# Fewer, wider small operations in a decode kernel with attention and MLP: remainder products, masks, bias row and quadrant copies

## The chip, the cores and the metric

The kernel runs on one core of a Trainium2 chip. The metric is the device time of one execution in microseconds (us), the median of several runs. Five engines work side by side, each through a fixed list of instructions: TensorE (PE, with weight loads as PEld), VectorE (DVE), ScalarE (ACT), GpSimd (POOL) and SyncE (SP), which here only issues transfers. They wait for each other through semaphores. Transfers from memory (HBM) to the on-chip buffer are issued on queues and moved by 16 DMA engines.

## What is computed

A decode step for 8 sequences: attention over the last 2048 positions of a cache of keys and values (32 query heads, 16 key/value heads of 128), an MLP with a hidden width of 4608, and a gate that mixes the two. From the reference, cut to what matters:

```python
def _A_ref(x, k_cache, v_cache, wq, wo):          # x: 8 x 1 x 576
    W = min(4096, max(256, Sk // 4))              # Sk = 8192, W = 2048
    q = (x @ wq).reshape(B, Sq, Hq, Dh)...        # wq: 576 x 4096
    k = jnp.repeat(k_cache[:, :, Sk - W:, :], rep, axis=1)
    v = jnp.repeat(v_cache[:, :, Sk - W:, :], rep, axis=1)
    scores = jnp.einsum("bhqd,bhkd->bhqk", q, k) * (Dh ** -0.5)
    p = _softmax(scores, axis=-1)
    o = jnp.einsum("bhqk,bhkd->bhqd", p, v)
    return ... @ wo                               # wo: 4096 x 576

def _B_ref(x, w1, b1, w2, b2):
    y = _layernorm(x, axis=-1)
    h = _gelu(jnp.einsum("bsd,df->bsf", y, w1) + b1)   # w1: 576 x 4608
    return jnp.einsum("bsf,fd->bsd", h, w2) + b2       # w2: 4608 x 576

x = A_x
g = _sigmoid((x * gate_w).sum(-1, keepdims=True))
return g * a + (1 - g) * b
```

The parts of the cache that are read are 8 x 16 x 2048 x 128 values of two bytes, 67.1 MB of keys and as much of values. The four weights are 20.1 MB together.

## The kernel before

The program is written as a plan: each operation is added with its engine, what it depends on, and an estimated cost. A small list scheduler inside the program uses the estimates to fix the order of each engine's list. Semaphore waits are then made from the dependencies.

```python
def add(self, eng, fn, deps=(), name=None, cost=0.1, after=(), prio=0): ...
def dma(self, eng, fn, semkey, nbytes, deps=(), name=None, after=(), prio=0): ...
# schedule(): of the ready operations, take the least (earliest start - 0.2 * prio, -prio, index)
    if op.is_dma:
        eng_free[op.eng] = est + op.cost                    # DMA_ISSUE = 0.35
        if op.nbytes < 65536:
            op.t1 = est + 0.4 + self.DMA_LAT                # DMA_LAT = 1.8: thought to be done at t1
        else:
            start = max(est + 0.4, dma_free)
            dma_free = start + op.nbytes / self.DMA_BW      # DMA_BW = 428e3 bytes per us
            op.t1 = dma_free + self.DMA_LAT
    else:
        op.t1 = est + op.cost                               # an operation may start 0.08 after what it needs
```

The inner dimension 576 is 4 x 128 + 64. The 64 rows that remain of wq and w1 are loaded two to a row pair, so that the two halves of the output columns lie on even and odd partitions; the input's remainder columns are spread with zeros to match (`xT[:, 4]` serves the first half of the heads, `xT[:, 5]` the second). Each block of 128 outputs takes five products:

```python
def q_fn(e):
    for hq in range(Hq):                                   # 32 heads
        out_ = ps[:, BK_Q, hq * 8: hq * 8 + 8]
        for t in range(4):
            ins = e.matmul(out_, wq_m[:, t, hq * 128:(hq + 1) * 128], xT[:, t, :], start=(t == 0), stop=False)
        c = hq % 16
        ins = e.matmul(out_, wq_r[:, c * 128:(c + 1) * 128], xT[:, 4 + hq // 16, :], start=False, stop=True)
# w1: the same, 36 blocks, weights read with a stride of 9, in lists of 6 blocks
o_hch.append(add("pe", fn, deps=dw1 + [o_yT], name="h_pe%d" % len(o_hch), cost=0.06 * 5 * len(fts), after=o_hch[-1:]))
```

Masks are made on VectorE before the inputs land: `own` by five memsets, `i2` by a memset and four copies, `i32` by four copies from an identity matrix.

The softmax of a group finds the maximum of 128 partitions x 512 scores (L597), brings the maxima of the four partition quadrants together (L600), and takes their maximum in three operations (L601 to L603):

```python
m01 = add("dve", ... max(k(MX), k(GA)) ...)
m23 = add("dve", ... max(k(GB_), k(GC_)) ...)
tt  = add("dve", ... max(k(M01), k(M23)) ...)
```

Keys come in 16 loads of 4.19 MB (`k_unit`), alternating between two buffers. A buffer is free when the two transposes of its content (L666) are done. Values come in 32 loads of 2.10 MB (`v_unit`) through five buffers, each free when its products (L711) are done. All these loads go out from SyncE in one fixed order:

```python
order = ("0 1 v 2 v 3 v 4 v v 5 v v 6 v v 7 v v 8 v v 9 v v 10 v v 11 v v 12 v v 13 v v 14 v 15 "
         "w w v v w w v v v v v v b m m m m")     # numbers: K; v: V; w: wo; b: output bias; m: w2
```

The products of a V load have the name `pv0` to `pv31`; item n holds `pv` 2n and 2n + 1. After each pair of V loads an item of attention output is evicted by ScalarE (L722), summed (L728), evicted again (L738) into one of two small buffers, scaled by GpSimd (L749), and at the end brought into place for the products with wo, by copies between partition quadrants (L761). The last four items have a burst of 16 copies each:

```python
ev = add("act", ... activation(out=o32[:, item % 2, :], in_=osrc, func=ACTF.Copy),
         deps=[prev] + ([oT_done[2 * item - 4], oT_done[2 * item - 3]] if item >= 2 else []), ...)
if i == NUQ - 9:
    place(slice(0, 8), slice(0, 6), list(oT_done.values()))
elif i >= NUQ - 8:
    c = (i % 8) // 2
    place_done[c] = place(slice(c, 8, 4), slice(6, 8), [oT_done[i - 1], oT_done[i]])

def place(ch, bs, deps):
    return [add("dve", ... tensor_copy(oT[32 * q:32 * q + 32, ch, j, bs], oN[32 * j:32 * j + 32, q, ch, bs]) ...)
            for j in range(4) for q in range(4)]
...
AccGroup("proj%d" % c, mms, place_done[c] + ds, cost=1.1)          # four groups, c = 0..3, 16 products each
```

The output bias b2 is loaded to 8 partitions and multiplied by a diagonal 8 x 8 matrix of 1 - g, split in a high and a low part (`ob`):

```python
o_obh = add("dve", lambda e: e.tensor_copy(ob[:, 0:8], dg[:, 8:16]), deps=[o_dgb], ...)
d = dma("sp", lambda e: e.dma_start(b2_sb, B_b2.partition_broadcast(8)), "b2", 65536, name="d_b2", after=last_dma[-1:])   # 65536: nbytes
o_m2.append(AccGroup("m2_b", [(ob[:, 0:8], b2_sb), (ob[:, 8:16], b2_sb)], [d, o_obl, o_obh], cost=0.6).op)
```

A w2 load needs a buffer that V products have freed: the four of them come after `pv27`, `pv28`, `pv29` and `pv30`. The group of wo products (`proj`) and those of w2 and b2 add up in one bank of PSUM; ScalarE evicts the half that wo and b2 have used when all of these groups are done (L807).

The last load of w2 comes in four pieces; their products (L555), one addition (L826) and the store of the output (L827) end the kernel.

Of the kernel before, what the change touches and what calls it, by code (L numbers as in the profile page):

```python
# [173 lines left out]
def held_matmul(nc, e, out, lhsT, rhs, start=False, stop=True, skip=False, tile_size=(128, 128), tile_position=(0, 0)):  # L174
    return e.add_instruction(mybir.InstMatmult(
        name=nc.get_next_instruction_name(), engine=mybir.EngineType.PE,
        ins=[e.lower_ap(rhs), e.lower_ap(lhsT)], outs=[e.lower_ap(out)],
        start_tensor_calc=start, stop_tensor_calc=stop, is_transpose=False, bass_skip_group_check=skip,
        tile_size=tile_size, tile_position=tile_position, ldweights=False))


def build_kernel(nc, A_x, A_k_cache, A_v_cache, A_wq, A_wo, B_x, B_w1, B_b1, B_w2, B_b2, gate_w, out):
# [24 lines left out]
    with ExitStack() as es:  # L207
# [39 lines left out]
        req("o32", 2 * 16, F32)  # L247
# [57 lines left out]
        b2_sb = view("b2", 8)  # L305
        u_sb, uh_sb, v1_sb, v2_sb = view("u"), view("uh"), view("v1"), view("v2")
        hT = view("hT").rearrange("p (t b) -> p t b", b=8)
        ob = view("ob", 8)
        ot32 = view("ot32", 8)
# [5 lines left out]
        o32 = view("o32").rearrange("p (u m) -> p u m", u=2)  # L315
# [60 lines left out]
        o_own0 = add("dve", lambda e: e.memset(view("own"), 0.0), name="own0", cost=0.1)  # L376
        o_own = [add("dve", (lambda a=a: lambda e: e.memset(view("own")[32 * a:32 * a + 32, a:a + 1], 1.0))(), deps=[o_own0], name="own%d" % a, cost=0.1) for a in range(4)]
# [67 lines left out]
        def b1ev_fn(e):  # L445
# [8 lines left out]
        o_obh = add("dve", lambda e: e.tensor_copy(ob[:, 0:8], dg[:, 8:16]), deps=[o_dgb], name="ob_hi", cost=0.12)  # L454
        o_ob32 = add("dve", lambda e: e.tensor_copy(ot32, ob[:, 0:8]), deps=[o_obh], name="ob_32", cost=0.12)
        o_obl = add("dve", lambda e: e.tensor_tensor(out=ob[:, 8:16], in0=dg[:, 8:16], in1=ot32, op=ALU.subtract), deps=[o_ob32], name="ob_lo", cost=0.12)

        o_i32 = []
        o_i20 = add("dve", lambda e: e.memset(view("i2"), 0.0), name="i2z", cost=0.1, prio=-1)
        o_i2 = [add("dve", (lambda q=q: lambda e: e.tensor_copy(i2[32 * q:32 * q + 32, :, q // 2, :], ident[32 * q:32 * q + 32, 32 * q:32 * q + 32].rearrange("p (r m) -> p r m", r=4)))(),  # L460
                    deps=[o_i20, o_ident], name="i2_%d" % q, cost=0.15, prio=-1) for q in range(4)]
        for q in range(4):
            o_i32.append(add("dve", (lambda q=q: lambda e: e.tensor_copy(i32[32 * q:32 * q + 32, :], ident[32 * q:32 * q + 32, 32 * q:32 * q + 32]))(),
                             deps=[o_ident, o_obl], name="i32_%d" % q, cost=0.15, prio=-1))


        def q_fn(e):
            ins = None
            for hq in range(Hq):
                out_ = ps[:, BK_Q, hq * 8: hq * 8 + 8]  # L470
                for t in range(4):
                    ins = e.matmul(out_, wq_m[:, t, hq * 128:(hq + 1) * 128], xT[:, t, :], start=(t == 0), stop=False)
                c = hq % 16
                ins = e.matmul(out_, wq_r[:, c * 128:(c + 1) * 128], xT[:, 4 + hq // 16, :], start=False, stop=True)
            return ins
# [23 lines left out]
        H_CH = 6  # L499
        o_hch = []  # L500
        for i0 in range(0, FT, H_CH):
            fts = list(range(i0, min(FT, i0 + H_CH)))
            def fn(e, fts=fts):
                ins = None
                for t in fts:
                    c, j = divmod(t, FJ)
                    out_ = ps[:, BK_H, t * 8: t * 8 + 8]
                    for kt in range(4):
                        lhsT = bass.AP(arena, offset=aoffs("RAW") + W1O + kt * F + FCW * c + j, ap=[[AST, 128], [FJ, 128]])
                        ins = e.matmul(out_, lhsT, yT[:, kt, :], start=(kt == 0), stop=False)  # L510
                    lhsT = bass.AP(arena, offset=aoffs("RAW") + W1O + 4 * F + FCW * (c % 2) + j, ap=[[AST, 128], [FJ, 128]])
                    ins = e.matmul(out_, lhsT, yT[:, 4 + c // 2, :], start=False, stop=True)  # L512
                return ins
            o_hch.append(add("pe", fn, deps=dw1 + [o_yT], name="h_pe%d" % len(o_hch), cost=0.06 * 5 * len(fts), after=o_hch[-1:]))
# [78 lines left out]
        def softmax(g):  # L593
            k = lambda i, n=1, parts=128, p0=0: sm[p0:p0 + parts, g, i:i + n]
            MX, GA, GB_, GC_, M01, M23, TT, NB, S = range(9)
# [5 lines left out]
            m01 = add("dve", lambda e: e.tensor_tensor(out=k(M01, 1, 32), in0=k(MX, 1, 32), in1=k(GA, 1, 32), op=ALU.max), deps=[sh[0]], name="m01_%d" % g, cost=0.16, prio=5)  # L601
            m23 = add("dve", lambda e: e.tensor_tensor(out=k(M23, 1, 32), in0=k(GB_, 1, 32), in1=k(GC_, 1, 32), op=ALU.max), deps=sh[1:], name="m23_%d" % g, cost=0.16, prio=5)  # L602
            tt = add("dve", lambda e: e.tensor_tensor(out=k(TT, 1, 32), in0=k(M01, 1, 32), in1=k(M23, 1, 32), op=ALU.max), deps=[m01, m23], name="t_%d" % g, cost=0.16, prio=5)  # L603
# [97 lines left out]
        def v_compute(i, s, d):  # L701
# [31 lines left out]
            if q % 2 == 1:  # L733
                hl = q // 2
                prev = u_sum[item]
                osrc = ps[:, BK_S, OC + 16 * (item % 2):OC + 16 * (item % 2) + 16]
                if item < Hkv - 1:
                    ev = add("act", lambda e: e.activation(out=o32[:, item % 2, :], in_=osrc, func=ACTF.Copy), deps=[prev] + ([oT_done[2 * item - 4], oT_done[2 * item - 3]] if item >= 2 else []), name="oev%d" % item, cost=0.25, prio=3)  # L738
                    o_item_ev[item] = ev
                    b6_r.append(ev)  # L740
                    eng, src_, deps = "pool", o32[:, item % 2, :], [ev, rg_done[g]]
                else:
                    eng, src_, deps = "dve", osrc, [prev, rg_done[g]]
                for t in (i - 1, i):
                    G, n = divmod(t, 8)

                    def om_fn(e, t=t, G=G, n=n):
                        dst = bass.AP(arena, offset=aoffs("oN") + 128 * (n % 2) + 8 * (n // 2) + 2 * G, ap=[[AST, 128], [1, 2], [32, 2], [64, 2]])
                        return e.tensor_tensor(out=dst, in0=src_[:, 8 * (t % 2):8 * (t % 2) + 8].rearrange("p (b l h) -> p b l h", b=2, l=2),  # L749
                                               in1=rg[:, g % 2, 8 * (t % 4):8 * (t % 4) + 8].rearrange("p (b l h) -> p b l h", b=2, l=2), op=ALU.mult)  # L750
                    oT_done[t] = add(eng, om_fn, deps=deps, name="oT%d" % t, cost=0.25, prio=9)
                if i == NUQ - 9:
                    place(slice(0, 8), slice(0, 6), list(oT_done.values()))
                elif i >= NUQ - 8:
                    c = (i % 8) // 2
                    place_done[c] = place(slice(c, 8, 4), slice(6, 8), [oT_done[i - 1], oT_done[i]])

        place_done = {}

        def place(ch, bs, deps):  # L760
            return [add("dve", (lambda j=j, q=q: lambda e: e.tensor_copy(oT[32 * q:32 * q + 32, ch, j, bs], oN[32 * j:32 * j + 32, q, ch, bs]))(), deps=deps, name="pl%d%d" % (j, q), cost=0.1, prio=2)  # L761
                    for j in range(4) for q in range(4)]
# [10 lines left out]
        def project():  # L773
            for c in range(4):
                mms, ds = [], []
                for j in range(4):
                    for ch in (c, c + 4):
                        dst, d = wo_here[ch // 2]
                        mms.append((oT[:, ch, j, :], dst[:, ch % 2, D * j:D * j + D]))
                        ds.append(d)  # L780
                AccGroup("proj%d" % c, mms, place_done[c] + ds, cost=1.1)
# [3 lines left out]
        def bias(i):  # L785
            d = dma("sp", lambda e: e.dma_start(b2_sb, B_b2.partition_broadcast(8)), "b2", 65536, name="d_b2", after=last_dma[-1:])
            last_dma.append(d)
            o_m2.append(AccGroup("m2_b", [(ob[:, 0:8], b2_sb), (ob[:, 8:16], b2_sb)], [d, o_obl, o_obh], cost=0.6).op)
# [103 lines left out]
```

## Time and profile before

| what | before |
|---|---|
| time, median of 3 runs | 366.11 us (366.08 to 366.67) |
| span of the profiled execution | 364.9 us |
| bytes read | 154.31 MB |
| transposes of K, L666 | 32 of 4424 ns |
| products of wq, w1 (main and remainder) | 128 + 32, 144 + 36 |
| copies between quadrants, L761 | 64 of 160 ns, 16 of 167 ns |

The span counts from the first to the last instruction. A row by stage has the length of the stage, then for each engine the busy time and, in brackets, how many instructions, then the granted TensorE clock as a share of full speed, the mean busy share of the 16 DMA engines, and what they moved in GB/s. The chain of waits is followed back from the last instruction, at each step to what released it. L666 is line 666 of the kernel.

### The profile page before, as it was taken

What the parts mean: (1) busy time and instruction counts of PE and PEld (TensorE: products, weight loads), DVE (VectorE), ACT (ScalarE), POOL (GpSimd) and SP (SyncE); (2) the same over time, 40 slices, a digit from 0 to 9 for tenths busy, and PEclk for the clock granted to TensorE, in tenths of its full rate; (3) what the DMA queues carried; (4) which work ended last, traced back from release to release, by engine and by line L of the source; (5) the groups of instructions that cost most, each with busy time, mean ns of one, the idle gap of its engine ahead of it and who ended that gap; (6) DMA issues with size and microseconds to landing.
All of it is one profiled execution on the core that took longest, in us unless ns stands there. A gap on an engine that the chain in (4) does not pass through costs nothing.

```text
span 364.9 us, 3980 instructions
## 1 busy us (share of the span) xinstructions
PE 239.4 (66%) x1679; PEld 115.0 (32%) x1679; DVE 226.5 (62%) x340; ACT 22.4 (6%) x53; POOL 17.4 (5%) x80
## 2 busy tenths in 40 slices
PE   0269684838498938274959484738959297577575
PEld 0159331312143414022423232214424133234232
DVE  4700995675999280759965362789781739777221
ACT  1010000000000000000100000001100000001000
POOL 5021000001000000010000000000000000000000
PEclk9999998778589969596996978676978796859899
DMA  9999999999999999999999999999999999999995
GB/s 376 435 404 451 406 451 411 451 432 415 445 426 443 420 436 431 424 438 424 436 426 440 422 442 420 439 422 438 424 436 444 426 410 436 425 431 429 431 425 222
DMA packets 9690, 154.58 MB, mean 424 GB/s; under 512 B 1052, under 2 KB 1220, under 8 KB 2888
## 3 DMA queue, kind: packets, MB, share of 16 engines
q1 hardware_dynamic: 9616, 154.29, 98.9%
q8 instruction: 13, 0.21, 0.2%
q10 hardware_dynamic: 56, 0.03, 0.0%
q14 instruction: 5, 0.04, 0.0%
HBM read 154.31 MB, written 0.01 MB: 423 GB/s over the span
## 4 chain that ended last, share of the span: by engine, by line
DMA 62%; DVE 24%; PE 11%; issue 1%; SPq 0%; DVEq 0%
DMA arena<-in_A_k_cache_dram 54%; DVE arena L666 18%; PE ps L678 6%; DMA arena<-in_A_v_cache_dram 5%; PE ps L711 4%; DMA arena<-in_B_w_dram 4%; DVE arena L639 3%; DVE arena L597 1%; DVE arena L631 1%; DVE arena L600 0%; DVE arena L606 0%; PE ps L612 0%; DVE arena L614 0%; PE ps L555 0%; SPq L798 0%
## 5 line engine op out<-in xcount | busy, mean ns | idle before, releaser
L666 DVE STREAM_TRANSPOSE arena<-arena 128x4096 f32<-128x4096 f32 x32 | 140.7, 4424 | 85.4 <-DMA arena<-in_A_k_cache_dram 85.0
L678 PE MATMUL ps<-arena 128*32 128x512 bf16 x512 | 141.7, 440 | 62.7 <-DVE arena L666 62.7
L678 PEld LDWEIGHTS ps<-arena 128*32 128x32 bf16 x512 | 52.3, 105 | 144.7 <-DVE arena L666 67.7
L711 PE MATMUL ps<-arena 128*32 128x512 bf16 x512 | 60.7, 453 | 23.8 <-DVE arena L602 18.6
L711 PEld LDWEIGHTS ps<-arena 128*32 128x32 bf16 x512 | 24.8, 110 | 50.4 <-issue 31.7
L639 DVE STREAM_TRANSPOSE arena<-arena 128x512 bf16<-128x512 bf16 x32 | 30.8, 1019 | 0.0
L728 PE MATMUL ps<-arena 128*128 128x16 f32 x128 | 17.0, 264 | 5.6 <-ACT arena L722 3.9
L761 DVE COPY arena<-arena 32x4 bf16<-32x4 bf16 (+1 forms) x80 | 12.9, 161 | 10.1 <-POOL arena L749 7.9
L728 PEld LDWEIGHTS ps<-arena 128*128 128x128 f32 x128 | 15.5, 191 | 11.5 <-ACT arena L722 9.6
L722 ACT ACTIVATE arena<-ps 128x512 f32<-128x512 f32 x16 | 9.6, 598 | 148.9 <-PE ps L711 148.9
L749 POOL TENSOR_TENSOR arena<-arena 128x8 bf16<-128x8 f32 x30 | 5.9, 231 | 229.9 <-ACT arena L738 229.9
L597 DVE TENSOR_REDUCE arena<-ps 128x1 f32<-128x512 f32 x8 | 5.5, 692 | 12.2 <-PE ps L678 12.1
L510 PE MATMUL ps<-arena 128*128 128x8 bf16 x144 | 10.9, 201 | 2.6 <-DMA arena<-in_B_w_dram 2.6
L608 ACT ACTIVATE arena<-ps,arena 128x512 bf16<-128x512 f32 x8 | 5.5, 687 | 107.4 <-DVE arena L606 107.4
L510 PEld LDWEIGHTS ps<-arena 128*128 128x128 bf16 x144 | 10.8, 157 | 3.1 <-DMA arena<-in_B_w_dram 3.1
L555 PE MATMUL ps<-arena 128*8 128x288 bf16 (+1 forms) x140 | 9.3, 288 | 3.6 <-DMA arena<-in_B_w_dram 3.4
L659 POOL TENSOR_TENSOR arena<-arena 128x32 bf16<-128x32 bf16 x32 | 6.5, 240 | 86.0 <-PE ps L678 76.9
L612 PE MATMUL ps<-arena 128*128 128x32 f32 x16 | 3.9, 328 | 8.6 <-DVE arena L611 8.6
L631 DVE TENSOR_SCALAR arena<-arena 128x512 bf16<-128x512 bf16 x32 | 9.0, 324 | 0.0
L425 PE MATMUL ps<-arena 8*128 8x8 bf16 x8 | 0.6, 170 | 11.0 <-DVE arena L398 7.0
L512 PE MATMUL ps<-arena 128*128 128x8 bf16 x36 | 7.2, 201 | 0.0
L555 PEld LDWEIGHTS ps<-arena 128*8 128x8 bf16 (+1 forms) x140 | 4.6, 85 | 7.8 <-DMA arena<-in_B_w_dram 4.9
(84 smaller groups left out, 77.8 us busy)
## 6 DMA issues: line engine op xcount, KB each, us to landing
arena<-in_A_k_cache_dram SPq DMA_DIRECT2D x16, 4096.0 KB, 25.2
arena<-in_A_v_cache_dram SPq DMA_DIRECT2D x32, 2048.0 KB, 24.3
arena<-in_B_w_dram SPq DMA_DIRECT2D x1, 4608.0 KB, 24.1
arena<-in_A_wo_dram SPq DMA_DIRECT2D x4, 1152.0 KB, 10.0
arena<-in_A_wq_dram SPq DMA_DIRECT2D x1, 4096.0 KB, 13.4
arena<-in_B_w_dram SPq DMA_DIRECT2D x3, 1296.0 KB, 18.9
arena<-in_B_w_dram SPq DMA_DIRECT2D x2, 432.0 KB, 12.2
arena<-in_B_w_dram SPq DMA_DIRECT2D x1, 576.0 KB, 25.2
```

What stands on the lines that cost most here:

```text
L510: ins = e.matmul(out_, lhsT, yT[:, kt, :], start=(kt == 0), stop=False)
L512: ins = e.matmul(out_, lhsT, yT[:, 4 + c // 2, :], start=False, stop=True)
L555: ins = e.matmul(ps[c:c + 8, BK_ACC, 0:JN], lhsT, rhs[:, JN * j:JN * j + JN], start=False, stop=True, skip_group_check=True, tile_position ...
L597: mx = add("dve", lambda e: e.tensor_reduce(out=k(MX), in_=ps[:, bank, :], axis=AXL.X, op=ALU.max), deps=[qk_done[g]], name="mx%d" % g, co ...
L631: return e.tensor_scalar(out=dst, in0=view("Pd").rearrange("p (s n) -> p s n", s=2), scalar1=amask[:, a:a + 1], scalar2=None, op0=ALU.mult)
L639: return e.transpose(dst, src)
L666: tr = add("dve", (lambda h=h, kb=kb: lambda e: e.transpose(bass.AP(arena_f, offset=foffs("KT") + kb * SE // 2, ap=[[AST // 2, 128], [4, 1 ...
L678: mm = e.matmul(ps[32 * c:32 * c + 32, 2 * (G % 2) + nb, :], qb[:, G % 2, n, 2 * h + ee, :], rhs, start=(h == 0 and t == 0), stop=(h == 1 ...
L711: mm = e.matmul(ps[c:c + 32, bk, :], PT[:, g % 2, 512 * q + 32 * t:512 * q + 32 * t + 32], slot(s)[:, 512 * t:512 * t + 512], start=(t < 2 ...
L722: u_ev[item] = add("act", lambda e: e.activation(out=EV[:, item % 2, :], in_=ps[:, bk, :].rearrange("p (r d j) -> p r j d", r=4, j=4), fun ...
L728: mm = e.matmul(ps[:, BK_S, OC + 16 * (item % 2):OC + 16 * (item % 2) + 16], EV[:, item % 2, 128 * r:128 * r + 128], i2[:, r, :, :].rearra ...
L761: return [add("dve", (lambda j=j, q=q: lambda e: e.tensor_copy(oT[32 * q:32 * q + 32, ch, j, bs], oN[32 * j:32 * j + 32, q, ch, bs]))(), d ...
```

## The change

It merges small operations. It is meant to shorten the instruction lists of TensorE and VectorE and to load less for the output bias.

- A remainder product takes 16 moving columns (both halves of `xT` or `yT`) and writes two output blocks at once, with the start flag; the eight main products of the two blocks follow. 16 products for wq and 18 for w1 are dropped.
- `own`, `i2` and `i32` are made by one, two and one reductions over the identity.
- The three maxima of a group become one reduction over four columns.
- b2 is loaded as one row; its factor is taken from the copy of 1 - g that lies on all partitions, later than before.
- The copies for the first three of the last four items are one burst of 16, after the third of them; the fourth keeps its own.
- Each item of attention output has its own small buffer, so that ScalarE need not wait for GpSimd to have read one.

```diff
 def q_fn(e):
-    for hq in range(Hq):
-        out_ = ps[:, BK_Q, hq * 8: hq * 8 + 8]
-        for t in range(4):
-            ins = e.matmul(out_, wq_m[:, t, ...], xT[:, t, :], start=(t == 0), stop=False)
-        ins = e.matmul(out_, wq_r[:, c * 128:(c + 1) * 128], xT[:, 4 + hq // 16, :], start=False, stop=True)
+    for c in range(Hq // 2):
+        both = ps[:, BK_Q, 0:Hq * 8].rearrange("p (s c b) -> p c s b", s=2, b=8)[:, c, :, :]
+        e.matmul(both, wq_r[:, c * 128:(c + 1) * 128], xT[:, 4:6, :], start=True, stop=False, skip_group_check=True)
+        for hq in (c, c + Hq // 2):
+            for t in range(4):
+                ins = e.matmul(ps[:, BK_Q, hq * 8: hq * 8 + 8], wq_m[:, t, ...], xT[:, t, :], start=False, stop=(t == 3), ...)
...  (w1 likewise)
-        H_CH = 6
+        H_CH = 3
-            o_hch.append(add("pe", fn, ..., cost=0.06 * 5 * len(fts), ...))
+            o_hch.append(add("pe", fn, ..., cost=0.06 * 9 * len(fts), ...))
...
-        o_own0 = add("dve", lambda e: e.memset(view("own"), 0.0), ...)
-        o_own = [add("dve", ... memset(view("own")[32 * a:32 * a + 32, a:a + 1], 1.0) ...) for a in range(4)]
+        o_own = [add("dve", lambda e: e.tensor_reduce(out=view("own"), in_=ident.rearrange("p (a i) -> p a i", a=4), axis=AXL.X, op=ALU.max), ...)]
...  (i2 and i32 likewise)
-        o_obh = add("dve", lambda e: e.tensor_copy(ob[:, 0:8], dg[:, 8:16]), deps=[o_dgb], ...)
+        o_obh = add("dve", lambda e: e.tensor_copy(ob[:, 0:8], gb[0:1, 8:16]), deps=[o_gb], ...)
-            d = dma("sp", lambda e: e.dma_start(b2_sb, B_b2.partition_broadcast(8)), "b2", 65536, ...)
+            d = dma("sp", lambda e: e.dma_start(b2_sb, B_b2.partition_broadcast(1)), "b2", D * 2, ...)
...
-            m01 = ...; m23 = ...; tt = ... max(k(M01), k(M23)) ...
+            tt = add("dve", lambda e: e.tensor_reduce(out=k(TT, 1, 32), in_=k(MX, 4, 32), axis=AXL.X, op=ALU.max), deps=sh, ...)
...
-                    ev = add("act", ... out=o32[:, item % 2, :] ..., deps=[prev] + ([oT_done[2 * item - 4], oT_done[2 * item - 3]] if item >= 2 else []), ...)
+                    ev = add("act", ... out=o32[:, item, :] ..., deps=[prev], ...)
...
-                    place(slice(0, 8), slice(0, 6), list(oT_done.values()))
-                elif i >= NUQ - 8:
-                    place_done[c] = place(slice(c, 8, 4), slice(6, 8), [oT_done[i - 1], oT_done[i]])
+                    place(0, 4, slice(0, 6), list(oT_done.values()))
+                elif i == NUQ - 3:
+                    place_done.append(place(0, 3, slice(6, 8), [oT_done[t] for t in range(NUQ - 8, NUQ - 2)]))
+                elif i == NUQ - 1:
+                    place_done.append(place(3, 4, slice(6, 8), [oT_done[i - 1], oT_done[i]]))
...
-                AccGroup("proj%d" % c, mms, place_done[c] + ds, cost=1.1)
+                AccGroup("proj%d" % c, mms, place_done[c // 3] + ds, cost=1.1)
```

More of the change, by code (lines that the diff above doesn't have):

```diff
@@ L171 @@
 ARENA_BASE = 16512
[L174 to L179, printed above, removed]
 def build_kernel(nc, A_x, A_k_cache, A_v_cache, A_wq, A_wo, B_x, B_w1, B_b1, B_w2, B_b2, gate_w, out):
@@ L246, in build_kernel @@
         req("rg", 2 * 32, F32)
-        req("o32", 2 * 16, F32)
+        req("o32", (Hkv - 1) * 16, F32)
         req("EV", 2 * 512, F32)
@@ L304, in build_kernel @@
         b1T = view("b1T")
-        b2_sb = view("b2", 8)
+        b2_sb = view("b2", 1)
         u_sb, uh_sb, v1_sb, v2_sb = view("u"), view("uh"), view("v1"), view("v2")
         hT = view("hT").rearrange("p (t b) -> p t b", b=8)
-        ob = view("ob", 8)
-        ot32 = view("ot32", 8)
+        ob = view("ob", 1)
+        ot32 = view("ot32", 1)
         gb = view("gb")
@@ L314, in build_kernel @@
         rg = view("rg").rearrange("p (g m) -> p g m", g=2)
-        o32 = view("o32").rearrange("p (u m) -> p u m", u=2)
+        o32 = view("o32").rearrange("p (u m) -> p u m", m=16)
         oN = view("oN").rearrange("p (q c b) -> p q c b", q=4, c=8)
@@ L375, in build_kernel @@
             o_selb.append(add("pool", fn, deps=[o_ident], name="selb%d" % he, cost=0.3))
-        o_own0 = add("dve", lambda e: e.memset(view("own"), 0.0), name="own0", cost=0.1)
-        o_own = [add("dve", (lambda a=a: lambda e: e.memset(view("own")[32 * a:32 * a + 32, a:a + 1], 1.0))(), deps=[o_own0], name="own%d" % a, cost=0.1) for a in range(4)]
+        o_own = [add("dve", lambda e: e.tensor_reduce(out=view("own"), in_=ident.rearrange("p (a i) -> p a i", a=4), axis=AXL.X, op=ALU.max), deps=[o_ident], name="own", cost=0.25)]
         o_am = add("dve", lambda e: e.tensor_reduce(out=amask, in_=ident.rearrange("p (q a h) -> p a q h", q=16, a=4), axis=AXL.XY, op=ALU.add), deps=[o_ident], name="amask", cost=0.25)
@@ L453, in build_kernel @@
         o_gb = add("dve", lambda e: e.tensor_copy(gb, ps[:, BK_X, 384:400]), deps=[o_gp], name="gb_ev", cost=0.15)
-        o_obh = add("dve", lambda e: e.tensor_copy(ob[:, 0:8], dg[:, 8:16]), deps=[o_dgb], name="ob_hi", cost=0.12)
+        o_obh = add("dve", lambda e: e.tensor_copy(ob[:, 0:8], gb[0:1, 8:16]), deps=[o_gb], name="ob_hi", cost=0.12)
         o_ob32 = add("dve", lambda e: e.tensor_copy(ot32, ob[:, 0:8]), deps=[o_obh], name="ob_32", cost=0.12)
-        o_obl = add("dve", lambda e: e.tensor_tensor(out=ob[:, 8:16], in0=dg[:, 8:16], in1=ot32, op=ALU.subtract), deps=[o_ob32], name="ob_lo", cost=0.12)
+        o_obl = add("dve", lambda e: e.tensor_tensor(out=ob[:, 8:16], in0=gb[0:1, 8:16], in1=ot32, op=ALU.subtract), deps=[o_ob32], name="ob_lo", cost=0.12)
@@ L458, in build_kernel @@
         o_i32 = []
[L459 to L464, printed above, removed]
+        o_i2 = [add("dve", (lambda u=u: lambda e: e.tensor_reduce(out=i2[:, :, u, :], in_=ident[:, 64 * u:64 * u + 64].rearrange("p (a r m) -> p r m a", a=2, r=4), axis=AXL.X, op=ALU.max))(),
+                    deps=[o_ident], name="i2_%d" % u, cost=0.2, prio=-1) for u in range(2)]
@@ L467, in q_fn @@
+        o_i32.append(add("dve", lambda e: e.tensor_reduce(out=i32, in_=ident.rearrange("p (a m) -> p m a", a=4), axis=AXL.X, op=ALU.max), deps=[o_ident, o_obl], name="i32", cost=0.25, prio=-1))
         def q_fn(e):
             ins = None
-            for hq in range(Hq):
-                out_ = ps[:, BK_Q, hq * 8: hq * 8 + 8]
-                for t in range(4):
-                    ins = e.matmul(out_, wq_m[:, t, hq * 128:(hq + 1) * 128], xT[:, t, :], start=(t == 0), stop=False)
-                c = hq % 16
-                ins = e.matmul(out_, wq_r[:, c * 128:(c + 1) * 128], xT[:, 4 + hq // 16, :], start=False, stop=True)
+            for c in range(Hq // 2):
[3 more added lines that the diff above has]
+                    for t in range(4):
+                        ins = e.matmul(ps[:, BK_Q, hq * 8: hq * 8 + 8], wq_m[:, t, hq * 128:(hq + 1) * 128], xT[:, t, :], start=False, stop=(t == 3), skip_group_check=True)
@@ L496, in build_kernel @@
         o_q4 = add("act", q4_fn, deps=[o_selp], name="q4_ev", cost=1.2)
-        H_CH = 6
+        H_CH = 3
         o_hch = []
-        for i0 in range(0, FT, H_CH):
-            fts = list(range(i0, min(FT, i0 + H_CH)))
+        for i0 in range(0, FT // 2, H_CH):
+            fts = list(range(i0, i0 + H_CH))
             def fn(e, fts=fts):
@@ L506, in fn @@
                     c, j = divmod(t, FJ)
[L507 to L512, printed above, removed]
+                    both = ps[:, BK_H, 0:FT * 8].rearrange("p (s t b) -> p t s b", s=2, b=8)[:, t, :, :]
+                    lhsT = bass.AP(arena, offset=aoffs("RAW") + W1O + 4 * F + FCW * c + j, ap=[[AST, 128], [FJ, 128]])
+                    e.matmul(both, lhsT, yT[:, 4:6, :], start=True, stop=False, skip_group_check=True)
+                    for s in range(2):
+                        for kt in range(4):
+                            lhsT = bass.AP(arena, offset=aoffs("RAW") + W1O + kt * F + FCW * (c + 2 * s) + j, ap=[[AST, 128], [FJ, 128]])
+                            at = (t + s * FT // 2) * 8
+                            ins = e.matmul(ps[:, BK_H, at: at + 8], lhsT, yT[:, kt, :], start=False, stop=(kt == 3), skip_group_check=True)
                 return ins
-            o_hch.append(add("pe", fn, deps=dw1 + [o_yT], name="h_pe%d" % len(o_hch), cost=0.06 * 5 * len(fts), after=o_hch[-1:]))
+            o_hch.append(add("pe", fn, deps=dw1 + [o_yT], name="h_pe%d" % len(o_hch), cost=0.06 * 9 * len(fts), after=o_hch[-1:]))
         o_hp = o_hch[-1]
@@ L594, in softmax @@
             k = lambda i, n=1, parts=128, p0=0: sm[p0:p0 + parts, g, i:i + n]
-            MX, GA, GB_, GC_, M01, M23, TT, NB, S = range(9)
+            MX, GA, GB_, GC_, TT, NB, S = range(7)
             bank = g % 4
@@ L600, in softmax @@
                 sh.append(add("dve", (lambda i=i, dst=dst: lambda e: e.tensor_copy(k(dst, 1, 32), k(MX, 1, 32, 32 * i)))(), deps=[mx], name="mg%d_%d" % (g, i), cost=0.16, prio=5))
-            m01 = add("dve", lambda e: e.tensor_tensor(out=k(M01, 1, 32), in0=k(MX, 1, 32), in1=k(GA, 1, 32), op=ALU.max), deps=[sh[0]], name="m01_%d" % g, cost=0.16, prio=5)
-            m23 = add("dve", lambda e: e.tensor_tensor(out=k(M23, 1, 32), in0=k(GB_, 1, 32), in1=k(GC_, 1, 32), op=ALU.max), deps=sh[1:], name="m23_%d" % g, cost=0.16, prio=5)
-            tt = add("dve", lambda e: e.tensor_tensor(out=k(TT, 1, 32), in0=k(M01, 1, 32), in1=k(M23, 1, 32), op=ALU.max), deps=[m01, m23], name="t_%d" % g, cost=0.16, prio=5)
+            tt = add("dve", lambda e: e.tensor_reduce(out=k(TT, 1, 32), in_=k(MX, 4, 32), axis=AXL.X, op=ALU.max), deps=sh, name="t_%d" % g, cost=0.16, prio=5)
             nbs = []
@@ L737, in v_compute @@
                 if item < Hkv - 1:
-                    ev = add("act", lambda e: e.activation(out=o32[:, item % 2, :], in_=osrc, func=ACTF.Copy), deps=[prev] + ([oT_done[2 * item - 4], oT_done[2 * item - 3]] if item >= 2 else []), name="oev%d" % item, cost=0.25, prio=3)
+                    ev = add("act", lambda e: e.activation(out=o32[:, item, :], in_=osrc, func=ACTF.Copy), deps=[prev], name="oev%d" % item, cost=0.25, prio=3)
                     o_item_ev[item] = ev
                     b6_r.append(ev)
-                    eng, src_, deps = "pool", o32[:, item % 2, :], [ev, rg_done[g]]
+                    eng, src_, deps = "pool", o32[:, item, :], [ev, rg_done[g]]
                 else:
@@ L752, in v_compute, with place @@
                 if i == NUQ - 9:
-                    place(slice(0, 8), slice(0, 6), list(oT_done.values()))
-                elif i >= NUQ - 8:
-                    c = (i % 8) // 2
-                    place_done[c] = place(slice(c, 8, 4), slice(6, 8), [oT_done[i - 1], oT_done[i]])
[L758 to L762, printed above, removed]
+                    place(0, 4, slice(0, 6), list(oT_done.values()))
[3 more added lines that the diff above has]
+                    place_done.append(place(3, 4, slice(6, 8), [oT_done[i - 1], oT_done[i]]))
+        place_done = []
+        def place(c0, c1, bs, deps):
+            ops = []
+            for j in range(4):
+                for q in range(4):
+                    dst = oT[32 * q:32 * q + 32, :, j, bs].rearrange("p (a c) b -> p a c b", a=2)[:, :, c0:c1, :]
+                    src = oN[32 * j:32 * j + 32, q, :, bs].rearrange("p (a c) b -> p a c b", a=2)[:, :, c0:c1, :]
+                    ops.append(add("dve", (lambda dst=dst, src=src: lambda e: e.tensor_copy(dst, src))(), deps=deps, name="pl%d%d" % (j, q), cost=0.1, prio=2))
+            return ops
         def wo_chunk(i):
@@ L780, in project @@
                         ds.append(d)
-                AccGroup("proj%d" % c, mms, place_done[c] + ds, cost=1.1)
+                AccGroup("proj%d" % c, mms, place_done[c // 3] + ds, cost=1.1)
         o_m2, o_ac = [], []
         def bias(i):
-            d = dma("sp", lambda e: e.dma_start(b2_sb, B_b2.partition_broadcast(8)), "b2", 65536, name="d_b2", after=last_dma[-1:])
+            d = dma("sp", lambda e: e.dma_start(b2_sb, B_b2.partition_broadcast(1)), "b2", D * 2, name="d_b2", after=last_dma[-1:])
             last_dma.append(d)
```

## The prediction

> **What bounds the kernel now.** First the head of the page: engine totals, slices, and the DMA queues.
>
> ```profile
> PE 239.4 (66%) x1679; PEld 115.0 (32%) x1679; DVE 226.5 (62%) x340; ACT 22.4 (6%) x53; POOL 17.4 (5%) x80
> ...
> DMA  9999999999999999999999999999999999999995
> ...
> q1 hardware_dynamic: 9616, 154.29, 98.9%
> ```
>
> No compute engine is busy over two thirds of the span; the DMA digit is 9 in 39 of 40 slices, and one queue takes 98.9% of what 16 engines can give. Next the same sums by stage, to see whether the queue is short of work anywhere (last columns: DMA share, GB/s).
>
> ```profile
> 36.60:75.00 38.40, 26.34 (x118) 10.62 (x117) 28.50 (x12) 0.89 (x2) 0.00 (x0) 0.91 1.00 429
> 75.00:115.00 40.00, 27.04 (x160) 12.41 (x161) 34.84 (x49) 3.12 (x8) 2.41 (x12) 0.79 1.00 430
> 115.00:300.00 185.00, 126.05 (x708) 55.67 (x707) 114.41 (x109) 10.15 (x26) 5.14 (x26) 0.81 1.00 431
> 300.00:345.00 45.00, 29.92 (x201) 13.77 (x197) 31.53 (x96) 4.69 (x12) 1.56 (x8) 0.81 1.01 430
> 345.00:358.00 13.00, 9.87 (x112) 5.10 (x112) 5.07 (x32) 0.60 (x1) 0.00 (x0) 0.88 0.99 422
> ```
>
> The transfers never pause: the kernel is bound by 154.3 MB at 0.43 MB/us (359 us), plus the start and what follows the last byte. The chain of waits names transposes (18%) and products (6%) too, but each is followed by a transfer that was queued long before, so that time runs beside the transfers. A change can then matter in two ways only: bytes, or the order of work, if a load is issued so late that the queue runs dry, or if computing is left over after the last byte. So third I read the timeline from 328 us on, cut to SyncE, TensorE and the bursts of copies.
>
> ```profile
> 328.69 1.42 SPq L697 DMA_DIRECT2D arena<-in_A_v_cache_dram  x2
> 330.15 0.53 SPq L786 DMA_DIRECT2D arena<-in_B_b_dram  x1
> ```
> ```profile
> 321.94 3.60 PE L711 MATMUL ps<-arena 128*32 128x512 bf16 x16 [4.72 <-DVE arena L602]
> ...
> 330.54 1.90 PE L711 MATMUL ps<-arena 128*32 128x512 bf16 x16
> ...
> 333.13 1.06 PE L728 MATMUL ps<-arena 128*128 128x16 f32 x8 [0.69 <-ACT arena L722]
> ...
> 350.07 1.90 PE L711 MATMUL ps<-arena 128*32 128x512 bf16 x16 [1.11 <-DMA arena<-in_A_v_cache_dram]
> ...
> 351.90 0.29 PE L555 MATMUL ps<-arena 8*8 8x288 bf16 x4
> ...
> 354.06 3.03 DVE L761 COPY arena<-arena 32x4 bf16<-32x4 bf16 x16
> ```
>
> The reader is to see three things. The row of b2 is issued at 330.15, just behind the last V load. The last V load lands at 350.0, where its products (350.07) wait for a DMA. And the bias products (351.90, four of 8x288) stand on TensorE behind those last V products. A view of the waits of SyncE adds that the four w2 loads wait for V products:
>
> ```profile
> SPq L798 <- PE ps L711: 16.7, 4, 6.0
> ```
>
> [...] the list of DMA issues has the last w2 piece, 144 KB, landing 12.7 us after its issue. [...] the 16 V products took 3.60 us at 321.94, clock 0.50, and 1.90 at full clock. [...] L761 takes 160 ns for 32x4 and 167 for 32x48.
>
> **The change part by part.** Remainder rows: 160 wq products ran from 18.05 to 22.48, 27.7 ns each, and 180 w1 products from 26.93 to 37.85, 60.7 ns each. I take a product of 16 columns to cost as one of 8. 16 x 27.7 + 18 x 60.7 ns is 1.5 us less. It is hidden: the K load behind wq is issued at 22.51 with 5.2 MB (12 us) still queued, and the addition behind w1 (41.01) waits for a transpose.
>
> Masks: 5.0 us of small VectorE operations become four reductions; one like them (L378) takes 0.29, so 3.8 us go. Most stood before 10.07 us, where VectorE was idle for 4.15 us: hidden. Maxima: 126 + 140 + 147 ns become one of some 150 in 8 groups, 2 us in all, in front of transposes whose loads are issued with at least 1.2 us to spare: hidden. Quadrant copies: four bursts of 3.03 us become two, 6.1 us less. The price is that three of the four wo groups wait for item 14. The buffers for o32 lift a wait that the profile never names. The bias row takes 8.1 KB of 154.3 MB, 0.02 us. By sums of work, 1.5 us of TensorE and 11.9 us of VectorE go, and 0.02 us of it is on the path: 366.1.
>
> **What moves.** The size in the bias load's plan entry falls from 65536 to 1152 bytes, and the planner treats the two differently: a transfer below 65536 is thought to land 2.2 us after its issue, a larger one only when all earlier bytes have gone. The planner orders by thought times, so I followed them by hand, for the order alone. In its account group 6's last small transposes end near 322.1; V products 24, a softmax sum, V products 25 and 26 follow to about 329.0, the last V load goes out at once and b2 0.35 later, at 329.4: thought to land at 331.6. After the sum of item 12, V products 27 run from 330.9 to 332.8. Next in line are the bias products, ready; V products 28 are thought ready only at 335.6, when their load lands. So the bias products now stand **behind V products 27 and ahead of the sum of item 13 and V products 28 to 31**. Before, they were thought ready near 350.5, which is where the trace has them.
>
> TensorE takes its list in order. In truth b2 [...] lands near 350.0. TensorE should thus stand still from 332.4 to 350.0, with four sets of V products, and the w2 loads that their buffers hold up, behind it. From there the end is a chain; I add it with the trace's durations.
>
> - To 354.9: bias products, sum of item 13, V products 28. At full clock 0.3 + 1.06 + 1.9[...].
> - To 356.8: V products 29, 1.9.
> - To 358.5: eviction and sum of item 14, 1.76 (342.15 to 343.91 before).
> - To 362.3: eviction and scaling 0.72, one burst of copies 3.03; V products 30 lie beside it.
> - To 363.9: two wo groups of 16 products, 0.8 each. By the same reckoning the planner puts them ahead of V products 31.
> - To 365.8: V products 31, 1.9.
> - To 367.6: eviction and sum of item 15, 1.76.
> - To 370.9: scaling and the last burst, 3.36 (353.73 to 357.09).
> - To 373.6: the fourth wo group and the last two w2 chunks, 52 products at 52 ns (34 took 1.76 at 356.27).
> - To 375.6: addition and store, 1.95 as before (362.95 to the end at 364.9).
>
> The w2 loads are beside this: issued at about 332.5, 354.9, 356.8 and 360.5, the last lands near 367, ahead of its use. The span would grow by 10.7 us, and the time from 366.1 to **376.8 us**.
>
> **Rivals.** First, the order does not bite: b2[...] overtakes, or my hand order is wrong and the bias products stay at the end. Then nothing is on the path and the time is 366.0. For it: the page gives no landing time for b2. Against: the 144 KB piece that took 12.7 us in order, and a margin of 2.8 us in the planner's account (332.8 against 335.6). Second, the removed work pays: 24% of the chain is VectorE, and a share of 13 us might bring 361 to 364. Against it: 300 us at an unbroken 430 GB/s. Third, the bias products land even ahead of V products 27 (the thought times are 0.8 us apart): then the first w2 load is late as well and one more set of products joins the chain, 379 to 380. Fourth, the stall comes but the end is shorter, since [...] the groups pass one another otherwise: 371 to 374.
>
> **Range and chances.** I give the stall 0.87; within it the chain is good to about 3 us, so 373.5 to 379.8 should hold 8 in 10. A loss of 2% begins at 373.4: chance 0.84. A gain of 2% would need 358.8, just what the bytes alone take: 0.01. The rest, within 2%, is 0.15.
>
> **What would show it.** Right: TensorE idle from about 332 to 350, released by the load of the bias; L555 with 1x288 as the first products after it; SyncE's second w2 load issued near 355 instead of 337; DMA digits below 9 in the last three slices; middle stretches still at 430 GB/s; VectorE near 215 us busy. Wrong: V products 28 near 335 and last weights at 362 would say that the order did not change, or that b2 lands early.

## The result, and the profile after

| | before | after |
|---|---|---|
| time, median of 4 runs | 366.23 us (366.08 to 366.67) | 375.74 us (373.88 to 376.59) |
| ratio of the times | | 1.0251 (95% interval 1.0211 to 1.0291) |
| span of the profiled execution | 364.9 us | 374.1 us |
| TensorE products / VectorE instructions | 1679 / 340 | 1645 / 282 |

The changed kernel does less work and takes 2.5% longer. The prediction was 376.8 us, in a range of 373.5 to 379.8.

The head of the changed kernel's page:

```profile
PE 236.3 (63%) x1645; PEld 114.2 (31%) x1645; DVE 216.6 (58%) x282; ACT 22.3 (6%) x53; POOL 17.4 (5%) x80
...
DMA  9999999999999999999999999999999999999690
...
q1 hardware_dynamic: 9602, 154.28, 96.5%
```

VectorE is busy 9.9 us less and TensorE has 34 products fewer, and the bytes are the same but for 0.01 MB. The DMA digits are 9 up to the 37th slice, then 6, 9, 0: transfers first pause near 350 us, and are over well before the end. The same by stage (busy times of PE, PEld, DVE, ACT, POOL, then granted clock, DMA share, GB/s) shows which stage it is:

```profile
115.00:300.00 185.00, 123.63 (x697) 55.04 (x698) 111.93 (x99) 10.13 (x26) 5.12 (x26) 0.80 1.00 431
300.00:330.00 30.00, 20.10 (x111) 8.95 (x106) 25.84 (x58) 3.12 (x8) 0.77 (x4) 0.83 1.02 431
330.00:347.50 17.50, 1.90 (x16) 0.71 (x16) 0.00 (x0) 0.60 (x1) 0.00 (x0) 0.66 1.01 430
347.50:359.50 12.00, 9.30 (x68) 5.09 (x68) 2.63 (x16) 0.96 (x3) 0.78 (x4) 0.78 0.74 293
359.50:374.10 14.60, 11.26 (x160) 6.72 (x160) 3.28 (x19) 1.00 (x2) 0.00 (x0) 0.88 0.34 131
```

Up to 347.5 us the transfers run at 430 GB/s as before. From 330 to 347.5 TensorE does one set of 16 products and VectorE nothing at all, where before both were busy with V products and copies (11.81 and 8.14 us in the same stretch). The chain of waits of the changed kernel (start, length, what) names what they stood for, and the timeline what followed:

```profile
328.32 19.14 DMA arena<-in_B_b_dram
```
```profile
330.57 1.90 PE L699 MATMUL ps<-arena 128*32 128x512 bf16 x16 [1.88 <-DMA arena<-in_A_v_cache_dram]
...
347.50 0.41 PE L545 MATMUL ps<-arena 1*8 1x288 bf16 x4 [15.03 <-DMA arena<-in_B_b_dram]
347.84 1.89 PE L716 MATMUL ps<-arena 128*128 128x16 f32 x8
349.66 4.25 PE L699 MATMUL ps<-arena 128*32 128x512 bf16 x32
...
356.39 3.10 DVE L755 COPY arena<-arena 32x12 bf16<-32x12 bf16 x16 [27.33 <-POOL arena L737]
359.54 2.09 PE L545 MATMUL ps<-arena 128*8 128x288 bf16 x32 [2.04 <-DVE arena L755]
361.43 2.00 PE L699 MATMUL ps<-arena 128*32 128x512 bf16 x10
...
366.17 3.03 DVE L755 COPY arena<-arena 32x4 bf16<-32x4 bf16 x16
369.26 2.86 PE L545 MATMUL ps<-arena 128*8 128x288 bf16 x52 [1.12 <-DVE arena L755]
...
372.17 0.45 DVE L820 TENSOR_TENSOR arena<-ps,arena 40x288 bf16<-40x288 f32 x1 [2.96 <-PE ps L545]
```

The bias row, 1152 bytes, is issued at 328.32 and takes 19.14 us. Its four products (`1x288`) come right after V products 27, wait 15.03 us, and hold up V products 28 to 31 and all that hangs on them: V products 28 start at 349.66, where in the kernel before they started at 335.39, when their load was in. The last 52 products at 369.26 wait for the copies, and no longer for weights: the end is a chain of computing.

### The profile page after: what moved, and what is told of

Read it like the earlier page. It is cut to its first block, busy times and chain, and to the rows that moved or that the text cites. A ratio compares the mean times of both kernels' runs of the same rounds, so it can differ in the third digit from the quotient of the medians.

```text
span 374.1 us, 3841 instructions
## 1 busy us (share of the span) xinstructions
PE 236.3 (63%) x1645; PEld 114.2 (31%) x1645; DVE 216.6 (58%) x282; ACT 22.3 (6%) x53; POOL 17.4 (5%) x80
## 4 chain that ended last, share of the span: by engine, by line
DMA 58%; DVE 27%; PE 12%; issue 2%; SPq 0%; ACT 0%; POOL 0%; DVEq 0%
DMA arena<-in_A_k_cache_dram 53%; DVE arena L654 19%; PE ps L666 5%; DMA arena<-in_B_b_dram 5%; PE ps L699 4%; DVE arena L627 3%; PE ps L545 1%; DVE arena L755 1%; PE ps L716 1%; DVE arena L619 1%; DVE arena L587 1%; DVE arena L594 0%; DVE arena L590 0%; ACT arena L710 0%; DVE arena L602 0%
## 5 line engine op out<-in xcount | busy, mean ns | idle before, releaser
L666 PE MATMUL ps<-arena 128*32 128x512 bf16 x512 | 140.2, 436 | 65.6 <-DVE arena L654 65.6
L699 PE MATMUL ps<-arena 128*32 128x512 bf16 x512 | 60.1, 457 | 20.8 <-DVE arena L627 18.9
L755 DVE COPY arena<-arena 32x48 bf16<-32x48 bf16 (+2 forms) x48 | 7.9, 164 | 28.5 <-POOL arena L737 27.3
L716 PE MATMUL ps<-arena 128*128 128x16 f32 x128 | 17.8, 271 | 4.7 <-ACT arena L710 3.0
L716 PEld LDWEIGHTS ps<-arena 128*128 128x128 f32 x128 | 16.3, 199 | 10.5 <-ACT arena L710 8.3
L502 PE MATMUL ps<-arena 128*128 128x8 bf16 x144 | 9.8, 201 | 0.0
L502 PEld LDWEIGHTS ps<-arena 128*128 128x128 bf16 x144 | 9.8, 158 | 0.0
L600 PEld LDWEIGHTS ps<-arena 128*128 128x128 f32 x16 | 2.6, 203 | 11.2 <-DVE arena L599 10.0
## 6 DMA issues: line engine op xcount, KB each, us to landing
arena<-in_B_w_dram SPq DMA_DIRECT2D x1, 576.0 KB, 25.1
```

Source lines behind the costliest of these rows:

```text
L502: ins = e.matmul(ps[:, BK_H, at: at + 8], lhsT, yT[:, kt, :], start=False, stop=(kt == 3), skip_group_check=True)
L666: mm = e.matmul(ps[32 * c:32 * c + 32, 2 * (G % 2) + nb, :], qb[:, G % 2, n, 2 * h + ee, :], rhs, start=(h == 0 and t == 0), stop=(h == 1 ...
L699: mm = e.matmul(ps[c:c + 32, bk, :], PT[:, g % 2, 512 * q + 32 * t:512 * q + 32 * t + 32], slot(s)[:, 512 * t:512 * t + 512], start=(t < 2 ...
L716: mm = e.matmul(ps[:, BK_S, OC + 16 * (item % 2):OC + 16 * (item % 2) + 16], EV[:, item % 2, 128 * r:128 * r + 128], i2[:, r, :, :].rearra ...
L755: ops.append(add("dve", (lambda dst=dst, src=src: lambda e: e.tensor_copy(dst, src))(), deps=deps, name="pl%d%d" % (j, q), cost=0.1, prio=2))
```

## The experiments

Theory A is the prediction's: the bias products moved forward in TensorE's list, because the planner is told 1152 bytes and believes such a load lands in 2.2 us; TensorE then waits for the row. Theory B: the merged quadrant copies bring the wo groups late, and that is what lengthens the end. Theory C: the place of the products hurts in itself. Theory D: the transfers that pause near 350 us are what costs.

**One number put back in the changed kernel.** Only the size told to the planner; the row stays one row.

```diff
-B_b2.partition_broadcast(1)), "b2", D * 2, name="d_b2"
+B_b2.partition_broadcast(1)), "b2", 65536, name="d_b2"
```

> The changed kernel with one number put back: the size that the planner is told for the bias row is 65536 again (the load itself stays one row of 1152 bytes). Theory A (the bias products were placed ahead of V products 28 to 31 because the planner thinks a small load lands 2.2 us after its issue, and TensorE waits for the row): the bias products go back behind V products 31, no wait of 15 us is left, and the time is that of the kernel before, 366.0 us (365.6 to 366.4). Theory B (the merged quadrant copies bring the wo groups late, and that lengthens the end): nearly all of the loss stays, 373 to 376 us.

Measured: 366.19 us, ratio to before 0.9997 (0.9989 to 1.0006). The whole loss hangs on that number. It also gives the worth of everything else in the change: nothing measurable, although VectorE is busy 216.8 us instead of 226.5. The merged copies are still there, and two of the three wo groups that wait for them run at 349.19, after their burst. The bias products (`1x288`) are back behind V products 31, in front of the w2 products that run at 355.44. The end does not notice the merging, as its last products again wait for weights:

```profile
349.19 1.50 PE L545 MATMUL ps<-arena 128*8 128x288 bf16 x32 [2.05 <-DVE arena L755]
...
355.44 2.59 PE L545 MATMUL ps<-arena 1*8 1x288 bf16 x40
...
362.26 0.65 PE L545 MATMUL ps<-arena 128*8 128x288 bf16 x6 [0.17 <-DMA arena<-in_B_w_dram]
```

**The same number alone, in the kernel before.**

```diff
-B_b2.partition_broadcast(8)), "b2", 65536, name="d_b2"
+B_b2.partition_broadcast(8)), "b2", D * 2, name="d_b2"
```

> The kernel before with one number changed: the planner is told 1152 bytes for the load of the bias, which stays at 8 rows. Nothing of the change's own work is in it. Theory A: the same wait appears, bias products behind V products 27, and the time is 376 to 379 us, a little over the changed kernel, since now each burst of copies stands in line between V products; TensorE waits from about 332 to between 347.5 us (where the single row landed) and 350 us [...]. Theory B: 366 us, since the copies are not merged here.

Measured: 378.23 us, ratio 1.0341 (1.0309 to 1.0373). Nothing of the change's work is in this kernel, and it loses more than the whole change does. Its eight rows end the wait later than the single row:

```profile
350.06 0.40 PE L555 MATMUL ps<-arena 8*8 8x288 bf16 x4 [17.82 <-DMA arena<-in_B_b_dram]
```

**The row loaded at the start, the products left in place.**

```diff
+d_b2 = dma("act", lambda e: e.dma_start(b2_sb, B_b2.partition_broadcast(1)), "b2", D * 2, name="d_b2", after=[d_b1])
 ...
-o_m2.append(AccGroup("m2_b", [...], [d, o_obl, o_obh], cost=0.6).op)
+o_m2.append(AccGroup("m2_b", [...], [d_b2, o_obl, o_obh], cost=0.6, after=pv_hist[27:28]).op)
```

> The changed kernel with the bias row loaded at the start on ScalarE's queue instead of behind the last V load; the bias products are held at the place they have in the changed kernel, behind V products 27 (TensorE's list is the same). Theory A (it is the wait for the row, not the place): 366.0 us (365.5 to 366.5), the bias products run near 332.5 without a wait. Theory C (the place itself, or the shape with one row, upsets the end): 372 us or more. Theory B: 373 to 376.

Measured: 366.15 us, ratio 0.9998 (0.9990 to 1.0006). The products stand where they stand in the changed kernel, and cost nothing once the row is there:

```profile
330.54 2.81 PE L700 MATMUL ps<-arena 128*32 128x512 bf16 x16 [2.09 <-DMA arena<-in_A_v_cache_dram]
333.28 0.41 PE L546 MATMUL ps<-arena 1*8 1x288 bf16 x4
```

Theory C falls. A slower clock costs nothing here either: in this run the next three sets of V products took 3.60 us each (granted clock 0.50), and the final addition started at 362.88, against 362.95 in the kernel before, for these products lie beside the transfers. In the changed kernel, where the work after the wait lies on the chain, the slower clock does count: at a granted clock of 0.50 from 347.5 to 351.7 and 0.81 from there to 354.4, the sum of item 13 took 1.89 us instead of 1.06, and V products 28 and 29 together 4.25 instead of 3.80.

**The merging of the copies undone.**

```diff
-elif i == NUQ - 3:
-    place_done.append(place(0, 3, slice(6, 8), [oT_done[t] for t in range(NUQ - 8, NUQ - 2)]))
-elif i == NUQ - 1:
-    place_done.append(place(3, 4, slice(6, 8), [oT_done[i - 1], oT_done[i]]))
+elif i >= NUQ - 8:
+    c = (i % 8) // 2
+    place_done.append(place(c, c + 1, slice(6, 8), [oT_done[i - 1], oT_done[i]]))
 ...
-AccGroup("proj%d" % c, mms, place_done[c // 3] + ds, cost=1.1)
+AccGroup("proj%d" % c, mms, place_done[c] + ds, cost=1.1)
```

> The changed kernel with the merging of the quadrant copies undone (four bursts of 16 for the last four items), and the small size still told for the bias row. Theory A: the wait stays, and the end is no shorter: each of the first three bursts now stands in the chain between V products, 376.6 us (375.5 to 378), some 1 us over the changed kernel. Theory B: the merging was at fault, so 366 to 370 us.

Measured: 375.71 us, ratio 1.0261 (1.0245 to 1.0277), the changed kernel's time. Theory B falls with this run and the first. My expectation of 1 us more was also off: the burst of item 13 (350.79 to 353.82) lies beside V products 28. V products 31 do start later after the row, 14.5 us instead of 13.9, but they then run alone in 1.89 us, where in the changed kernel they run interleaved with the third wo group and take 2.7. One makes up for the other.

**The later w2 loads freed from the V products.**

```diff
+if ci in (1, 2):
+    dst = view("KT")[:, (ci - 1) * SE:(ci - 1) * SE + FJ * D]      # transposed keys, free since 313 us
+    free, key = qk_half[29 + ci], "m%d" % ci
+else:
+    s = take_slot(); dst = slot(s)[:, 0:FJ * D]; free, key = slot_free[s], "s%d" % s
```

> The changed kernel, wait for the bias row and all, but the second and third w2 load go to the buffer of the transposed keys, which is free since 313 us, so that they are issued right behind the first and no longer wait for V products 28 and 29; the fourth waits for V products 28 instead of 30. TensorE's list is the same. Theory A as predicted (the end is a chain of computing behind the wait; the late w2 loads lie beside it): the same time as the changed kernel, 375.7 us (374.9 to 376.3), with the last w2 bytes moved some 5 us sooner. Theory D (the queue that ran dry between 351 and 354 us is what costs, since the kernel is bound by its bytes): 371 to 373 us.

Measured: 375.98 us, ratio 1.0256 (1.0230 to 1.0281). The transfers no longer pause, as the same stretch of the two kernels shows, first the changed kernel and then this one:

```profile
351.70:354.40 2.70, 2.21 (x24) 0.80 (x16) 0.00 (x0) 0.45 (x1) 0.00 (x0) 0.81 0.34 73
```
```profile
351.70:354.40 2.70, 2.60 (x24) 0.90 (x16) 0.00 (x0) 0.06 (x1) 0.00 (x0) 0.66 1.01 430
```

From 73 GB/s to 430, and the time is the same. The weights were all in by 362 us instead of some 365.6, about 3.5 us sooner and not 5 as expected; that did not matter either. The pause in the slices is real and costs nothing: theory D falls, for this kernel.

**The row issued one V load earlier, and two.** The bias products are held behind V products 27, and the wo groups are planned where they were (second pair of lines), so TensorE's list is the changed kernel's in both.

```diff
-         "w w v v w w v v v v v v b m m m m")
+         "w w v v w w v v v v v b v m m m m")     # e6;  e7: "... v v v v b v v m m m m"
 ...
+... cost=0.6, after=pv_hist[27:28]).op)
 ...
-            if kind == "B":
+            if kind == "M" and i == 0:
                 project()
```

> The changed kernel with the bias row issued one V load earlier, between V loads 30 and 31; the bias products are held behind V products 27 and TensorE's list is that of the changed kernel. Theory A (time follows the landing of the row one for one): a V load is 4.9 us of the queue, so the row lands near 342.7 instead of 347.5 and the time is 371 us (370 to 372). Theory C (the place of the products costs, not the landing): 375.7 us. If only the dry queue costs: 368 us or less.

> The same with the bias row issued two V loads earlier, between V loads 29 and 30. Theory A: the row lands near 338; the chain behind it would end at 364.6 us of span, just about where the transfers end by themselves (364.9), so the loss is all but gone: 366.4 us (366.0 to 367.2). Were the cost proportional to the wait of TensorE (5.5 of 15 us left), it would be 369.6 us.

Measured: 370.90 us (ratio 1.0132, 1.0115 to 1.0148) and 366.44 us (1.0008, 0.9994 to 1.0022). The wait for the row and, two V loads earlier, the last products:

```profile
343.18 0.41 PE L545 MATMUL ps<-arena 1*8 1x288 bf16 x4 [10.90 <-DMA arena<-in_B_b_dram]
```
```profile
338.50 0.41 PE L545 MATMUL ps<-arena 1*8 1x288 bf16 x4 [5.99 <-DMA arena<-in_B_b_dram]
...
362.31 0.66 PE L545 MATMUL ps<-arena 128*8 128x288 bf16 x6 [0.16 <-DMA arena<-in_B_w_dram]
```

Set beside the other runs, the starts from the trace of one run, the time as the median:

| kernel | row's products start | final addition starts | between | time |
|---|---|---|---|---|
| row two V loads earlier | 338.50 | 363.01 | 24.5 | 366.44 |
| row one V load earlier | 343.18 | 368.64 | 25.5 | 370.90 |
| changed kernel | 347.50 | 372.17 | 24.7 | 375.74 |
| w2 loads freed | 347.49 | 372.57 | 25.1 | 375.98 |
| four bursts | 347.85 | 372.30 | 24.5 | 375.71 |
| before, small size (8 rows) | 350.06 | 375.33 | 25.3 | 378.23 |

The end follows the landing of the row at a distance of 25 us, within half a microsecond either way, whatever else differs between these six. (In the second row of the table the traced run took 371.87 us, 1 us over its median; its V products 28 and 29 took 5.02 us.) At 338.5 that chain and the weights arrive together: the last products wait only 0.16 us for weights, and the loss is gone, though TensorE still waits 5.99 us for the row. So the cost is not the wait, but by how much the chain behind it passes the end of the transfers. The run with freed w2 loads says the same: there V products 27 took 3.60 us, so TensorE waited 13.41 us instead of 15.03 for a row that came at the same moment, and the time was the same.

**Two pieces for the last w2 load instead of four,** in the kernel with the row loaded at the start, to look for a version ahead of both.

```diff
-cuts = [0, 3, 6, 8, 9] if ci == FC - 1 else [0, FJ]
+cuts = [0, 6, 9] if ci == FC - 1 else [0, FJ]
```

> The changed kernel with the row loaded at the start (366.15 us as it ran), and the last w2 load cut in two pieces (6 and 3 of 9) instead of four, to see whether anything is left at the end for a version that beats both. [...] more products are left after the last piece: 18 x 0.06 against 12 x 0.06 us or so. I expect 366.1 us (365.7 to 366.5), no gain outside the noise. If short pieces were what holds the last stretch at 0.82 of the DMA share, 365.6 us.

Measured: 366.35 us, ratio 1.0005 (0.9991 to 1.0019): nothing gained. No version here beats the kernel before; those that put the bias row right equal it (366.15 to 366.44).

## Why the prediction was right

**The bound.** Right: the middle stretches stay at 428 to 431 GB/s, and removing 9.9 us of VectorE and 34 products changed nothing when the order was put right (366.19 us).

**The removed work is hidden.** Right in each part that the trace can show. A remainder product of 16 columns took 175 ns against 168 for one of 8, and the two sets of products ran in 4.00 and 9.89 us instead of 4.43 and 10.92, 1.46 us less against my 1.5. The reduction of the maxima took 145 ns, the merged burst 3.10 us. VectorE lost 9.9 us where I had 11.9: I took two bursts and the masks with the gaps in them (3.03 us for 16 copies of 160 ns, 2.56 us busy; 5.0 us of masks, 4.6 busy), which makes 1.3 us of the difference. The rest is not explained; none of it reached the end. The third K load went out at 45.87 us, against 45.81 before.

**The order.** Right: the bias products stand behind V products 27, ahead of the sum of item 13. The experiments with the planner's number show that it alone puts them there. The 2.8 us of margin were thus enough, in a reckoning by hand.

**The landing.** I had 350.0, the moment of the last V load; that a single row comes with that load was an estimate. It was 347.5. With eight rows the wait ended at 350.06. The packets that the traces keep show the difference: the eight rows of the kernel before with the small size start between 346.66 and 349.42 (between 346.81 and 349.48 in the kernel before itself), and the wait ended 0.64 us after the last of them; the single row starts at 346.95, and the wait ended 0.55 us later. The queue as a whole was no earlier, as the last packets of V start at 348.8 and 349.0 in the two runs. So the single row started 2.1 us ahead of the last packets of V in its run (346.95 against 349.0). What sets how early a single row comes is not shown.

**The chain.** I had 23.6 us from the landing to the final addition; it took 24.7. The first part was near (the burst ended 12.0 us after the landing, against 12.3; the slower clock, 0.50 up to 351.7, added 1.4 us, from 0.41, 1.89 and 4.25 us where full clock gives 0.29, 1.06 and 3.80, against the 1.6 us that my step to 354.9 holds above its sum at full clock, an estimate). The two wo groups took 0.3 us more than planned, and the part from V products 31 on was 1 us longer than its terms, since the products of V 31 and of the third wo group run interleaved and the former end at 364.1, 2.7 us after they start, and not 1.9. The final addition thus came at 372.2 instead of 373.6 (-2.5 + 1.1 = -1.4 us), and the span was 374.1 instead of 375.6: those two terms make up the difference. They have opposite signs, so the total came nearer than its parts: that much is luck.

**The w2 loads.** Issued at 332.5, 353.1, 353.9 and 357.5 against my 332.5, 354.9, 356.8 and 360.5, and beside the chain as said; the run with freed loads confirms it. One sign was off: of the last three DMA digits (6, 9, 0) I had expected all below 9.

**The rivals.** Overtaking of the whole queue and a gain from the removed work did not happen. V products 27 did stay ahead of the bias. Of the fourth rival the shorter end came true, by 1.4 us (the final addition at 372.2 instead of 373.6), with the row 2.5 us early, but not its time of 371 to 374 us.

## What to carry to other kernels

In a kernel bound by its transfers, ask of a change first what it does to the order of the lists and only then what work it removes: 10 us of removed VectorE work were worth nothing, and one number in a cost estimate was worth 2.5%. The small load behind a full queue came late here: 1152 bytes took 19.14 us behind four V loads, and with one V load fewer ahead of it, then two, its products started 4.3 and another 4.7 us sooner (the bytes of a V load, 2.10 MB, are 4.9 us at 0.43 MB/us). TensorE took its list in order: V products 28 started at 349.66, behind the bias products, and at 335.48 with the size put back, when their load was in. So the consumer of such a load must not stand ahead of other work in the list, and these few bytes were best loaded at the start (366.15 us). When an engine waits long, look for where the chain behind the wait passes the end of the bound: here about 6 us of the wait were free (5.99 us cost nothing that can be measured), and after that the delay of the row counted in full: by the table, rows 4.7, 4.3 and 2.6 us later made the time 4.5, 4.8 and 2.5 us longer.

## What the runs showed that was not expected

A transfer of 1152 bytes took 19.14 us behind V loads 28 to 31 (8.4 MB, 19.5 us at 0.43 MB/us); that was foreseen, but one row came 2.6 us earlier than eight (347.50 against 350.06). The packets of the eight rows, of 51 ns each, were spread over 2.8 us (346.66 to 349.42). And TensorE at half clock (granted clock 0.50) through the whole of V products 28 to 30 (3.60 us a set instead of 1.90) left the time at 366.15 us.
